# Two x tiles of a fused attention and gated-MLP kernel: by one DMA transpose in place of a load and eight TensorE transposes

## The chip, the cores and the metric

One core of one Trainium2 chip. The metric is the time of one execution on the device, in microseconds (us). Each kernel is run several times; all runs that are compared here were in the fast, undisturbed state, except that the state of e8_before_again, a single run, is unknown. The runs e0 to e3, e4 to e7 and e8 to e11 were made on three different chips, each group beside runs of the kernel before on the same chip; a ratio is always to these. A profile is one execution with its trace; the span in it is about 1.7 us shorter than the time on the device.

Names used below: TensorE (PE, with its weight loads as PEld), VectorE (DVE), ScalarE (ACT), GpSimd (POOL), SyncE (SP). A "q" after an engine's name is its sequencer: SPq is SyncE issuing DMAs.

## The reference, cut to what matters

```python
# x: [1, 2048, 512] bf16.  g * A(x) + (1 - g) * B(x), g = sigmoid(x @ gate_w)
def _B_ref(x, w_in, w_sp, b_sp, w_out):          # the gated MLP
    z = gelu(x @ w_in)                           # w_in: [512, 1376]; two halves of 688
    z1 = z[..., :688]
    z2 = layernorm(z[..., 688:])
    g = einsum('ts,bsf->btf', w_sp, z2) + b_sp[None, :, None]
    return (z1 * g) @ w_out
def _A_ref(x, wqkv, w_phi, wo): ...              # linear attention, 32 heads of 16; w_phi folded into q and k
```

Every product with x needs x transposed (features on the partitions) as the stationary operand. x has 16 tiles of 128 rows.

## The kernel before

The head loads x tiles 0 to 3 plainly into `xs`, transposes them on TensorE through PSUM, and takes tiles 4 to 15 by DMA transposes into `xT`. The z2 half of `w_in` comes in five pieces; the order in which TensorE needs them in the head is slab 0 (first part), slab 1, slab 2, slab 3, slab 0 (second part).

```python
    nc.sync.dma_start(out=xs[:, 0, :], in_=x2[0:P, :])
    nc.scalar.dma_start(out=w_z2[:, 0, 0:HF], in_=w_in_v[:, 0, FH:FH + HF])     # slab 0, first part
    nc.sync.dma_start(out=xs[:, 1, :], in_=x2[P:2 * P, :])
    load_z2w(nc.scalar, 1)                                                      # slab 1
    nc.sync.dma_start(
        out=xs[:, 2:4, :], in_=x2[2 * P:4 * P, :].rearrange("(i p) d -> p i d", p=P))
    load_z2w(nc.scalar, 2)                                                      # slab 2
    nc.sync.dma_start(out=w_z2[:, 0, HF:FH], in_=w_in_v[:, 0, FH + HF:F])       # slab 0, second part
    load_z2w(nc.scalar, 3)                                                      # slab 3
    x_dma_T(4)                      # DMA transpose of 128 rows
    for h in range(2):
        nc.sync.dma_start(out=w_z1[:, 2 * h:2 * h + 2, :], ...)
    for i in range(5, 8):
        x_dma_T(i)
    for q in range(2, NCH):
        nc.sync.dma_start_transpose(out=xT[:, :, q * CH:(q + 1) * CH], ...)     # 512 rows each
    # ... all on SyncE, in this order: brow, wqkT (2 transposes), wphi (8), wv_sb (2), wspT (4 transposes)
```

```python
    def z2_first_two():             # z2 of tiles 0 and 1; TensorE's program order
        # ... warm-up matmuls, transposes of tiles 0 and 1, products with slabs 0 and 1
        gate_T()                    # a matmul that turns gate_w into column 688 of w_z2
        one(0, 2, 0)                # first product with slab 2
        one(1, 2, 0)
        for dt in range(1, 3):
            one(0, dt, 1)
            one(1, dt, 1)
        x_T(2, 0, NDT, pq_tile([P, NDT, P], BF16)[:, :, :])      # four transposes, one copy
        for tt in range(2):
            one(tt, 3, 0)           # slab 3
            one(tt, 0, 1)           # slab 0, second part
            one(tt, 3, 1)
            z2_out(tt, zps[tt])     # ScalarE: gelu out of PSUM; VectorE: statistics
        x_T(3, 0, NDT, pq_tile([P, NDT, P], BF16)[:, :, :])
    # then z2_tile(2), z2_tile(3), z1 of tiles 0 to 3, z2 and z1 of tiles 4 to 15;
    # among tiles 8 to 11 the first "fold": 64 small matmuls on wqkT and wphi
```

The softmax here doesn't subtract the row's maximum and nothing guards it: scores larger than these inputs give would overflow.

## Time and profile before

| | |
|---|---|
| time before, first three runs | 208.83 us median (208.50 to 208.91) |
| TensorE busy | 201.7 of 206.8 us |
| first z2 matmul of tile 2 | 8.72 us |
| first matmul of the attention stage | 45.48 us |

From the page of the kernel before, its busy line and its chain of work that ended last:

```profile
PE 201.7 (98%) x1526; PEld 120.9 (58%) x1544; DVE 129.5 (63%) x278; ACT 76.5 (37%) x123; POOL 45.4 (22%) x73
...
PE 94%; DMA 2%; ACT 1%; issue 1%; ACTq 0%; DVE 0%
```

The view of waits, for TensorE alone (who waited for whom: us in total, times, longest):

```profile
PE zp L221 <- PEq L585: 0.8, 1, 0.8
PE zp L190 <- DMA w_z<-in_B_w_in_dram: 0.3, 1, 0.3
```

So TensorE runs nearly without a break, and what is cut from it, or from its waits, at the head should come off the total, as long as nothing later absorbs it. The timeline of the head (start, length, engine, line, operation; L190 are z matmuls, L276 transposes of x, L205 the gelu out of PSUM):

```profile
6.00 0.20 PE L286 MATMUL pq<-ident,gaterow 128*128 128x4 bf16 x1
...
6.52 1.04 PE L190 MATMUL zp<-w_z,xT 128*128 128x344 bf16 x6 [0.32 <-DMA w_z<-in_B_w_in_dram]
...
7.40 0.39 PE L276 MATMUL pq<-ident,xs 128*128 128x128 bf16 x4
...
7.62 1.04 PE L190 MATMUL zp<-w_z,xT 128*128 128x344 bf16 x6
...
8.50 0.39 PE L276 MATMUL pq<-ident,xs 128*128 128x128 bf16 x4
...
8.72 3.38 PE L190 MATMUL zp<-w_z,xT 128*128 128x344 bf16 x22
10.09 0.74 ACT L205 ACTIVATE z2all<-zp 128x688 bf16<-128x688 f32 x1 [0.46 <-PE zp L190]
```

Read starts, not lengths: a group of four transposes is 0.39 us long, but the next z matmul starts 0.22 us after the group does. The 10.09 is the gelu of tile 2.

SyncE's issues in the same timeline, and the landing of two loads from the list of DMA issues in the window from 1.7 to 3.3 us (KB each, median us from issue to landing):

```profile
1.74 0.43 SPq L123 DMA_DIRECT2D xs<-in_A_x_dram  x1
...
2.21 0.47 SPq L126 DMA_DIRECT2D w_z<-in_B_w_in_dram  x1
...
3.47 1.29 SPq L130 DMA_TRANSPOSE xT<-in_A_x_dram  x1
...
5.93 3.81 SPq L130 DMA_TRANSPOSE xT<-in_A_x_dram  x3
```

```profile
w_z<-in_B_w_in_dram ACTq DMA_DIRECT2D x3, 172.0 KB, 4.7
xs<-in_A_x_dram SPq DMA_DIRECT2D x1, 256.0 KB, 5.2
```

### The profile page before, as it was taken

The page shows a single profiled execution, that of the slowest core. Times are in us where ns is not written, and L with a number is a line of the kernel's source. Part 1 is how long each engine was busy: PE and PEld are TensorE (multiplying, and loading weights), DVE is VectorE, ACT ScalarE, POOL GpSimd, SP SyncE. Part 2 cuts the span into 40 slices and gives each one's busy share as a digit, 9 for nine tenths or more (in the row PEclk, how much of TensorE's full clock was granted, in tenths as well). Part 3 has the DMA queues.
Part 4 walks back from the last instruction along what each step waited for, and adds up shares of the span by engine and source line. Part 5 has one row for each costly group of instructions (what it writes and reads, how often), then busy time and mean ns, then how long its engine had stood idle before and what let it go on. Part 6 is the DMA issues. An engine that isn't in the chain of part 4 may idle for free.

```text
span 206.8 us, 3948 instructions
## 1 busy us (share of the span) xinstructions
PE 201.7 (98%) x1526; PEld 120.9 (58%) x1544; DVE 129.5 (63%) x278; ACT 76.5 (37%) x123; POOL 45.4 (22%) x73
## 2 busy tenths in 40 slices
PE   8999999999999999999999999999999999999994
PEld 4666666655566555556565666555455555655642
DVE  3377656656977778879797788555466553633330
ACT  2665678786322232333323032222251126001322
POOL 5020202020532327243342422222204220200000
PEclk9999999999999999999999999999999999999999
DMA  5999499999996025991413229763564767453642
GB/s 181 278 224 177 102 242 203 250 174 279 165 290 138 3 38 123 290 118 27 89 26 66 51 38 104 142 123 72 107 158 89 79 104 190 55 104 73 128 90 78
DMA packets 89315, 27.22 MB, mean 132 GB/s; under 512 B 83184, under 2 KB 89296, under 8 KB 89296
## 3 DMA queue, kind: packets, MB, share of 16 engines
q1 hardware_dynamic: 86384, 24.28, 62.8%
q10 hardware_dynamic: 2880, 2.68, 4.0%
q8 instruction: 12, 0.20, 0.4%
q14 instruction: 7, 0.06, 0.1%
q0 software_dynamic: 32, 0.00, 0.0%
HBM read 4.41 MB, written 2.10 MB: 31 GB/s over the span
## 4 chain that ended last, share of the span: by engine, by line
PE 94%; DMA 2%; ACT 1%; issue 1%; ACTq 0%; DVE 0%
PE mm L445 36%; PE zp L190 17%; PE mm L350 13%; PE mm L484 8%; PE mm L390 7%; PE mm L482 7%; DMA w_z<-in_B_w_in_dram 2%; PE at L458 2%; PE kvacc L406 2%; PE mm L487 1%; PE zp L303 0%; ACT z1all L256 0%; ACT wq_p L310 0%; ACTq L117 0%; PE pq L276 0%
## 5 line engine op out<-in xcount | busy, mean ns | idle before, releaser
L445 PE MATMUL mm<-z2all,wspT 128*128 128x344 bf16 x512 | 79.9, 309 | 0.0
L445 PEld LDWEIGHTS <-wspT 128*128 128x128 bf16 x512 | 49.0, 98 | 25.7 <-issue 0.4
L190 PE MATMUL zp<-w_z,xT 128*128 128x344 bf16 (+1 forms) x256 | 39.3, 312 | 0.3 <-DMA w_z<-in_B_w_in_dram 0.3
L354 ACT ACTIVATE eq<-mm 128x512 bf16<-128x512 f32 x32 | 17.4, 594 | 51.3 <-PE mm L350 21.3
L358 DVE TENSOR_REDUCE zs<-eq 128x64 f32<-128x1024 bf16 x16 | 19.5, 1220 | 20.4 <-ACT eq L354 20.4
L190 PEld LDWEIGHTS <-xT 128*128 128x128 bf16 x256 | 24.8, 99 | 12.4 <-issue 0.4
L450 DVE SCALAR_TENSOR_TENSOR ucat<-mm,bT,z1all 128x344 bf16<-128x344 f32 x32 | 17.4, 543 | 21.9 <-PE mm L445 21.9
L367 POOL TENSOR_TENSOR eq<-eq,ratio 128x512 bf16<-128x512 bf16 x16 | 16.9, 1059 | 49.9 <-DVE ratio L366 41.7
L354 ACT ACTIVATE ek<-mm 128x512 bf16<-128x512 f32 x32 | 17.3, 600 | 27.4 <-PE mm L350 27.4
L498 ACT ACTIVATE ob<-mm,g_inv 128x512 bf16<-128x512 f32 (+1 forms) x16 | 10.9, 681 | 32.8 <-PE mm L487 28.0
L358 DVE TENSOR_REDUCE zs<-ek 128x64 f32<-128x1024 bf16 x16 | 19.3, 1209 | 2.8 <-ACT ek L354 2.8
L484 PE MATMUL mm<-wspT,uT 128*128 128x512 bf16 (+2 forms) x85 | 20.1, 366 | 0.0
L350 PEld LDWEIGHTS <-xT 128*128 128x128 bf16 x128 | 12.2, 98 | 13.2 <-PE mm L487 0.8
L367 POOL TENSOR_TENSOR ek<-ek,ratio 128x512 bf16<-128x512 bf16 x16 | 16.9, 1059 | 2.3 <-DVE ratio L366 1.8
L350 PE MATMUL mm<-wq_p,xT 128*128 128x512 bf16 x55 | 16.0, 379 | 0.5
L390 PE MATMUL mm<-wv_sb,xT 128*128 128x512 bf16 x64 | 16.4, 379 | 0.0
L350 PE MATMUL mm<-wk_p,xT 128*128 128x512 bf16 x61 | 16.1, 379 | 0.3
L482 PE MATMUL mm<-wspT,oT 128*128 128x512 bf16 (+2 forms) x62 | 15.6, 365 | 0.3
L208 DVE BATCH_NORM_STATS2 bn<-z2all 128x6 f32<-128x344 bf16 x32 | 14.9, 501 | 0.0
L205 ACT ACTIVATE z2all<-zp 128x688 bf16<-128x688 f32 x16 | 11.8, 744 | 6.9 <-PE zp L190 6.9
L256 ACT ACTIVATE z1all<-zp 128x688 bf16<-128x688 f32 x16 | 11.9, 744 | 5.1 <-PE zp L190 4.6
L484 PEld LDWEIGHTS <-uT 128*128 128x128 bf16 x85 | 8.1, 98 | 9.2
(72 smaller groups left out, 145.2 us busy)
## 6 DMA issues: line engine op xcount, KB each, us to landing
out_dram<-ob ACTq DMA_DIRECT2D x15, 128.0 KB, 1.7
wspT<-in_B_w_out_dram SPq DMA_DIRECT2D x2, 640.0 KB, 4.8
w_z<-in_B_w_in_dram SPq DMA_DIRECT2D x2, 344.0 KB, 4.3
w_z<-in_B_w_in_dram ACTq DMA_DIRECT2D x3, 172.0 KB, 4.7
wv_sb<-in_A_wqkv_dram SPq DMA_DIRECT2D x2, 256.0 KB, 3.5
wspT<-in_A_wo_dram SPq DMA_DIRECT2D x2, 256.0 KB, 3.8
xs<-in_A_x_dram SPq DMA_DIRECT2D x2, 128.0 KB, 2.6
xs<-in_A_x_dram SPq DMA_DIRECT2D x1, 256.0 KB, 5.2
```

The costliest lines, as they stand in the source:

```text
L190: nc.tensor.matmul(zp[:, j, 0:n], lhsT=xT[:, dt, tt * P:(tt + 1) * P], rhs=wt[:, dt, j * HF:j * HF + n], start=(dt == first), stop=(dt == ...
L208: nc.vector.bn_stats(out=bn6[:, tt, j, :], in_=z2v[:, j, :])
L256: nc.scalar.activation(out=z1all[:, tt, :].rearrange("p (j n) -> p j n", j=2), in_=zp[:, :, 0:HF], func=AF.Gelu_apprx_tanh,)
L350: nc.tensor.matmul(ps[:, :], lhsT=xT[:, dt, tt * P:(tt + 1) * P], rhs=w[:, dt, :], start=(dt == 0), stop=(dt == NDT - 1))
L354: nc.scalar.activation(out=e[:, :, a, :], in_=ps[:, :].rearrange("p (h f) -> p h f", f=DH), func=AF.Exp, scale=1.0 - 2.0 * a)
L358: nc.vector.tensor_reduce(out=z[:].rearrange("p h a -> p (h a)"), in_=e[:].rearrange("p h a f -> p (h a) f"), axis=AX.X, op=ALU.add,)
L367: nc.gpsimd.tensor_tensor(out=e[:, :, 1, :], in0=e[:, :, 1, :], in1=ratio[:, :, None].to_broadcast([P, H, DH]), op=ALU.mult)
L390: nc.tensor.matmul(v_ps[:, :], lhsT=xT[:, dt, tt * P:(tt + 1) * P], rhs=wv_sb[:, dt, :], start=(dt == 0), stop=(dt == NDT - 1))
L445: nc.tensor.matmul(gp[:, 0:HF], lhsT=wspT[:, st, tt * P:(tt + 1) * P], rhs=z2all[:, st, j * HF:(j + 1) * HF], start=(st == 0), stop=(st == ...
L450: nc.vector.scalar_tensor_tensor(out=ucat[tt % NU][:, c0 + j * HF:c0 + (j + 1) * HF], in0=gp[:, 0:HF], scalar=bT[:, tt:tt + 1], in1=z1all[ ...
L482: nc.tensor.matmul(acc, lhsT=oT[:, g, :], rhs=wo_t[:, g, c0:c1], start=(g == 0), stop=False)
L484: nc.tensor.matmul(acc, lhsT=uT[:, i + ft, :], rhs=w_main[i][:, ft, c0:c1], start=False, stop=False)
```

## The change

The intent: take 0.45 us of transposes off TensorE at the head, where it is the bound, and let the DMA queues do them beside it.

```diff
-    xs = early.tile([P, 4, D], BF16, name="xs")
+    xs = early.tile([P, 2, D], BF16, name="xs")
@@
-    nc.sync.dma_start(
-        out=xs[:, 2:4, :], in_=x2[2 * P:4 * P, :].rearrange("(i p) d -> p i d", p=P))
     load_z2w(nc.scalar, 2)
     nc.sync.dma_start(out=w_z2[:, 0, HF:FH], in_=w_in_v[:, 0, FH + HF:F])
     load_z2w(nc.scalar, 3)
-    def x_dma_T(i):
-        nc.sync.dma_start_transpose(out=xT[:, :, i * P:(i + 1) * P], in_=x2[i * P:(i + 1) * P, :])
-    x_dma_T(4)
+    def x_dma_T(i, n=1):
+        nc.sync.dma_start_transpose(out=xT[:, :, i * P:(i + n) * P], in_=x2[i * P:(i + n) * P, :])
+    x_dma_T(2, 2)
     # (the two w_z1 loads)
-    for i in range(5, 8):
+    for i in range(4, 8):
         x_dma_T(i)
@@ z2_first_two
-        x_T(2, 0, NDT, pq_tile([P, NDT, P], BF16)[:, :, :])
         for tt in range(2): ...
-        x_T(3, 0, NDT, pq_tile([P, NDT, P], BF16)[:, :, :])
```

## The prediction

> **What bounds the kernel now.** TensorE. The page's busy table has PE at 201.7 us of a 206.8 us span, and its chain that ended last is 94% PE. The list of waits for PE has two entries: 0.8 us at the start and 0.3 us (once) for a load of w_z at 6.52 us. So only PE time at the head, or a wait there, can change the total.
>
> **What the change removes.**
> - Eight TensorE transposes (x tiles 2 and 3) and their two PSUM copies. The groups show a transpose at 219 ns, but these overlap. The timeline gives the real cost: the first group starts at 7.40 us and the next z matmul at 7.62; the second at 8.50, the next z matmul at 8.72. That is 0.22 us each, 0.45 us together, all on the chain. It agrees with about 56 ns from start to start of warm 128-column matmuls (the Trainium skill, "TensorE: Matmul & The Clock Gate", section "Wait — 56ns, not 53.3ns?"): 4 x 56 = 0.22 us. The VectorE copies (0.42 and 0.41 us) are off the chain.
> - The 256 KB load of xs tiles 2 and 3, issued at 1.74 us, 5.2 us to landing, ahead of the last part of w_z on SyncE.
>
> **What it adds and moves.** One 256-row DMA transpose, SyncE's fourth DMA, at about 2.2 us. The first transpose DMA of before waited on SyncE for a w_z landing (0.8 us in SyncE's list of waits, start 3.47): it is the ninth DMA and reuses a semaphore. The new one is the eighth and should not wait. Issue took 1.27 us for 128 rows and 1.88 us for 512; I estimate 1.45 us, so issue ends near 3.7. The single transposes of tiles 4 to 7 end issue near 9.7 us, as before; the w_z1 loads go out about 1 us earlier.
>
> **When does it land?** Ahead of it are 944 KB of loads instead of 1200 KB. Transpose packets in the trace are 256 bytes and take about 18 ns; 1024 of them over 16 DMA engines are about 1.15 us (estimate). The loads of before moved their first 944 KB by about 5.3 us; adding 1.15 us and some 0.5 us from last packet to landing gives about 7.0 us. Plausible: 6.6 to 8.0. PE needs tile 2 at about 8.0 to 8.3 us, so I expect no wait, with a margin near 1 us.
>
> **A second gain.** DMA queues are served in turn, packet by packet (the Trainium skill, "DMA: Bandwidth & Descriptors", section "Queues, rings and completion order"). With small 256-byte packets later in place of xs 2 and 3, the w_z slab that PE waited for (landed 6.48) should land near 6.1, so the 0.3 us wait should mostly vanish: the gate matmul before it runs at 6.00. I count 0.15 us.
>
> **Later.** Downstream DMAs have slack: the last w_phi load lands at 24.5 us, its matmuls start at 27.5; the first w_sp quarter lands at 36.7, used at 48.1. Nothing should take the gain back.
>
> **Sum.** 208.83 - 0.45 - 0.15 = 208.2 us. Range 207.7 to 208.8. Faster over 2%: 0.01. Same: 0.98. Slower over 2%: 0.01.
>
> **What would show it.** The timeline: first z2 matmul of tile 2 at about 8.1 us instead of 8.72; the fourth SyncE issue at about 2.2 us, landing near 7.0; no PE wait for xT; the w_z wait at most 0.1 us; everything after earlier by a constant 0.6 us.
>
> **What would make it wrong.** The transpose landing after 8.2 us (PE waits, gain halved or lost); its packets delaying the third or fourth w_z slab (needed near 6.2 and 7.2 us; landed 6.48 and 7.44 before); a longer issue; or a later wait that absorbs the gain.

## The result, and the profile after

Ratios here are the mean time of one kernel's runs over the mean of the other's in the same rounds, so not quite the ratio of the medians quoted beside them.

| | before | after | ratio (95% interval) |
|---|---|---|---|
| first comparison, 4 and 4 runs | 208.67 | 207.80 | 0.9960 (0.9942 to 0.9979) |
| e0_after_again, 11 and 6 runs | 208.64 | 208.01 | 0.9968 (0.9948 to 0.9987) |
| e11_after_third, 11 and 6 runs | 208.34 | 207.76 | 0.9967 (0.9940 to 0.9994) |

The three ratios are worth 0.8, 0.7 and 0.7 us of 208.6 us. By the rule of 2% that is "same"; the gain is small, but it is there in all three. Single runs scatter: those of before from 207.90 to 209.39 us, those of the changed kernel from 207.03 to 208.70.

From the page after:

```profile
PE 202.2 (98%) x1536; PEld 120.3 (58%) x1536; DVE 128.8 (62%) x276; ACT 76.5 (37%) x123; POOL 45.4 (22%) x73
...
PE 95%; DMA 2%; ACT 1%; ACTq 0%; DVE 0%; issue 0%
```

PE's busy sum has not fallen although eight instructions are gone: the trace of before lacks some matmul records (1526 listed, 1536 after; the weight loads, 1544 and 1536, do show the eight), which is why starts are compared here and not sums.

TensorE's waits after:

```profile
PE zp L219 <- PEq L581: 0.8, 1, 0.8
PE zp L188 <- DMA w_z<-in_B_w_in_dram: 0.2, 1, 0.2
```

The timeline after (L188 are the z matmuls, L203 the gelu), then SyncE's issues and the landing of the new transpose:

```profile
6.00 0.18 PE L282 MATMUL pq<-ident,gaterow 128*128 128x4 bf16 x1
...
6.41 5.57 PE L188 MATMUL zp<-w_z,xT 128*128 128x344 bf16 x37 [0.23 <-DMA w_z<-in_B_w_in_dram]
...
9.53 0.74 ACT L203 ACTIVATE z2all<-zp 128x688 bf16<-128x688 f32 x1 [0.23 <-PE zp L188]
```

```profile
1.74 0.42 SPq L124 DMA_DIRECT2D w_z<-in_B_w_in_dram  x1
...
2.21 1.57 SPq L128 DMA_TRANSPOSE xT<-in_A_x_dram  x1
...
3.83 1.08 SPq L132 DMA_DIRECT2D w_z<-in_B_w_in_dram  x2
...
4.96 5.27 SPq L128 DMA_TRANSPOSE xT<-in_A_x_dram  x4
```

```profile
xT<-in_A_x_dram SPq DMA_TRANSPOSE x1, 5.7
```

From 6.41 us on, the z matmuls run without a break: no transposes, no wait for `xT`. Tile 2's gelu starts at 9.53 instead of 10.09 us, 0.56 us earlier: 0.11 because slab 2 released TensorE at 6.41 instead of 6.52, 0.45 because of the transposes. The attention stage's first matmul is at 44.93 instead of 45.48 us (TensorE's timelines of before and after, in this order), and the span is 0.5 us shorter.

```profile
45.48 0.81 PE L350 MATMUL mm<-wk_p,xT 128*128 128x512 bf16 x2
```

```profile
44.93 1.24 PE L346 MATMUL mm<-wk_p,xT 128*128 128x512 bf16 x5
```

In these two traces the whole difference arises before 8.2 us and is carried to the end unchanged.

But SyncE's transposes of tiles 4 to 7 end their issue at 10.23 us (4.96 + 5.27) instead of 9.75. That will matter below.

### The profile page after: what moved, and what is told of

The parts are those of the page before. It is cut to its first block, busy times and chain, and to the rows that moved or that the text cites. A ratio compares the mean times of both kernels' runs of the same rounds, so it can differ in the third digit from the quotient of the medians.

```text
span 206.3 us, 3946 instructions
## 1 busy us (share of the span) xinstructions
PE 202.2 (98%) x1536; PEld 120.3 (58%) x1536; DVE 128.8 (62%) x276; ACT 76.5 (37%) x123; POOL 45.4 (22%) x73
## 4 chain that ended last, share of the span: by engine, by line
PE 95%; DMA 2%; ACT 1%; ACTq 0%; DVE 0%; issue 0%
PE mm L441 36%; PE zp L188 17%; PE mm L346 14%; PE mm L480 8%; PE mm L478 7%; PE mm L386 7%; DMA w_z<-in_B_w_in_dram 2%; PE at L454 2%; PE kvacc L402 2%; PE mm L483 1%; PE zp L299 0%; ACT z1all L252 0%; ACT wq_p L306 0%; ACTq L117 0%; ACTq L120 0%; PE pq L299 0%
## 5 line engine op out<-in xcount | busy, mean ns | idle before, releaser
L188 PE MATMUL zp<-w_z,xT 128*128 128x344 bf16 (+1 forms) x256 | 38.9, 312 | 0.2 <-DMA w_z<-in_B_w_in_dram 0.2
L188 PEld LDWEIGHTS <-xT 128*128 128x128 bf16 x256 | 24.9, 98 | 12.4 <-issue 0.3
L478 PE MATMUL mm<-wspT,oT 128*128 128x512 bf16 (+2 forms) x68 | 16.6, 366 | 0.0
L203 ACT ACTIVATE z2all<-zp 128x688 bf16<-128x688 f32 x16 | 11.8, 744 | 6.3 <-PE zp L188 6.3
```

The costliest lines, as they stand in the source:

```text
L188: nc.tensor.matmul(zp[:, j, 0:n], lhsT=xT[:, dt, tt * P:(tt + 1) * P], rhs=wt[:, dt, j * HF:j * HF + n], start=(dt == first), stop=(dt == ...
L478: nc.tensor.matmul(acc, lhsT=oT[:, g, :], rhs=wo_t[:, g, c0:c1], start=(g == 0), stop=False)
```

## The experiments

The theories. **A**, that of the prediction: two parts, 0.45 us of TensorE time in the head and some tenths because slab 2 lands earlier, and nothing later takes them back. Rivals: **R1**, the gain is the lighter DMA head and the transposes hide behind it; **R2**, the gain is the two VectorE copies that vanish; **R3**, the new transpose has slack; **B**, there is a third source of gain, since the first medians differ by more than the traces. Theories **C** and **D** came up on the way.

This table has, for each trace, the times that the argument uses, read from starts and landings in the traces: when slab 2 landed, when TensorE began on it, when tile 2's first z2 matmul started, how long it was from there to the end of the last matmul, and the time of that run.

| trace | slab 2 landed | TensorE goes on | tile 2 starts | difference | tile 2 to last matmul | that run |
|---|---|---|---|---|---|---|
| before | 6.48 | 6.52 | 8.72 | 2.20 | 195.27 | 208.54 |
| e8_before_again | 5.64 | 5.78 | 8.29 | 2.52 | 195.26 | 208.09 |
| after | 6.37 | 6.41 | 8.16 | 1.75 | 195.26 | 208.00 |
| e0_after_again | 5.67 | 5.71 | 7.46 | 1.75 | 195.27 | 207.28 |
| e11_after_third | 6.01 | 6.05 | 7.80 | 1.75 | 195.51 | 207.89 |
| e1_idle_T | 6.08 | 6.12 | 8.32 | 2.20 | 195.26 | 208.12 |
| e2_idle_T_copies | 6.26 | 6.30 | 8.74 | 2.44 | 195.25 | 208.53 |
| e3_before_swap | 6.57 | 6.61 | 9.21 | 2.59 | 195.24 | 208.99 |
| e4_drop_T_only | 7.01 | 7.05 | 8.84 | 1.78 | 195.25 | 208.64 |
| e5_late | 7.46 | 7.51 | 10.91 | 3.40 | 195.29 | 210.73 |
| e6_split | 5.93 | 5.97 | 7.73 | 1.75 | 195.93 | 208.34 |
| e7_reorder_split | 5.74 | 5.78 | 7.53 | 1.75 | 196.26 | 208.48 |
| e9_split_chunk_late | 5.96 | 6.07 | 8.06 | 2.00 | 195.36 | 208.10 |
| e10_reorder_chunk_late | 5.25 | 5.66 | 7.56 | 1.90 | 195.24 | 207.50 |

From tile 2 to the end the kernel takes 195.24 to 195.29 us in ten of the fourteen traces, whatever the head did. So the head decides, except in e11, e6, e7 and e9.

The two traces of before and the three of the changed kernel, set against each other by their means: tile 2 starts 0.70 us earlier (8.50 and 7.81), as much as the measured gain. Of this, 0.09 us is an earlier start on slab 2 and 0.61 us a shorter stretch from there to tile 2: 0.45 of transposes, and 0.16 that is the mean of what e8 alone lost in it (see e8). With so few traces this is an account, not a measurement.

### The changed kernel again, twice: e0_after_again, e11_after_third

No edit.

> The changed kernel unaltered, for a tighter difference and a second trace. Theory A (eight transposes leave TensorE, 0.45 us, and the w_z wait shrinks by 0.1 us, everything else carried along): 0.55 us below before. Theory B (there is a further gain of 0.3 us somewhere, as the first medians, 0.87 us apart, suggest): 0.8 to 0.9 us below before. Tile 2's first z matmul again near 8.16 us and the 256-row transpose landing near 7.9 us.

> The changed kernel once more, in the same rounds as the two versions above, to compare with them. 0.6 to 0.9 us below before; w_phi lands at 24.7 to 25.4 us, 1.6 us ahead of the fold; tile 2's transpose lands 0.1 to 0.6 us ahead of need.

Measured: ratios 0.9968 and 0.9967, as in the table above. Tile 2 starts at 7.46 and 7.80 us, not again at 8.16: the landing of slab 2 differs by 0.7 us between executions of one kernel. The transpose landed at 7.18 and 7.71 us, 0.28 and 0.10 us before tile 2's first matmul. In e11 nothing was left: tile 2's weight load, which in after and e0 starts 0.145 us ahead of its matmul (8.02 and 7.32 us), started only at 7.75, 0.055 us ahead, just in time for the matmul. The gain of 0.7 us lies between theories A (0.55) and B (0.8 to 0.9), and the intervals hold both, so the times do not decide. The traces need no third source: the first profiled run of the changed kernel was its slowest of four, with a late head. In e11 w_phi landed at 26.66 us, where 24.7 to 25.4 was expected, 0.04 us after the fold had begun; that trace lost time there (see theory D).

### Transposes put back on TensorE: e1_idle_T, e2_idle_T_copies

```diff
+    def idle_T(i):
+        tp = pq_tile([P, NDT, P], BF16)
+        for dt in range(NDT):
+            nc.tensor.transpose(tp[:, dt, :], xs[:, i, dt * P:(dt + 1) * P], ident[:, :])
+        # e2 only:
+        with tc.high_priority():
+            nc.vector.tensor_copy(out=spare[:, :, i * P:(i + 1) * P], in_=tp[:, :, :])
@@ z2_first_two, where x_T(2, ...) and x_T(3, ...) stood before
+        idle_T(0)
+        idle_T(1)
```

> The changed kernel with eight TensorE transposes put back where they were, into PSUM that nobody reads; TensorE's program is then that of before. Theory A: 0.45 us slower than the changed kernel, so 0.1 us below before. Rival R1 (the gain is the lighter DMA head, transposes on TensorE hide): as fast as the changed kernel. Rival R2 (the gain is the VectorE copies that vanish): as fast as the changed kernel too, and the next run then slower.

> As e1_idle_T, and the two 128x512 VectorE copies put back as well, into a spare tile; the programs of TensorE and VectorE are those of before and only the DMAs differ. Theory A: equal to e1_idle_T within 0.1 us, 0.1 us below before. Rival R2 (copies on VectorE cost): 0.3 us or more slower than e1_idle_T.

Measured: e1 208.17 us (ratio to before 0.9981, 0.9962 to 1.0000), e2 208.37 us (0.9988, 0.9969 to 1.0008); the changed kernel in the same rounds 208.01 us. By means, e1 and e2 are 0.26 and 0.43 us above the changed kernel and 0.42 and 0.26 us below before. Taken together, their twelve runs are 0.35 us above the changed kernel's six and 0.34 us below before's eleven, each good to about 0.3 us by the scatter of the runs (95%). The timeline of e1:

```profile
6.12 1.04 PE L188 MATMUL zp<-w_z,xT 128*128 128x344 bf16 x6 [0.48 <-DMA w_z<-in_B_w_in_dram]
...
6.99 0.39 PE L285 MATMUL pq<-ident,xs 128*128 128x128 bf16 x4
...
8.32 3.67 PE L188 MATMUL zp<-w_z,xT 128*128 128x344 bf16 x24
```

From 6.12 to 8.32 us is 2.20 us again, as before; without the transposes it is 1.75. R1 falls: the transposes do not hide, they cost 0.45 us of TensorE in the trace, and the times agree, within their scatter. R2 is not supported: e2 with the copies is 0.16 us above e1, which the scatter covers, and e2's trace has 2.44 us because the first two matmuls of that stretch took 445 and 447 ns instead of 307: TensorE's clock was released only at 6.81 us in that execution.

What e1 and e2 keep of the change is its DMAs alone. That is worth 0.3 us on average, though each run's own interval just reaches or includes no gain at all. So the lighter DMA head is likely a part of the gain; what the runs refuse is that it is the whole.

### Only the order of two loads: e3_before_swap

```diff
-    nc.sync.dma_start(out=xs[:, 2:4, :], ...)
     load_z2w(nc.scalar, 2)
     nc.sync.dma_start(out=w_z2[:, 0, HF:FH], ...)
+    nc.sync.dma_start(out=xs[:, 2:4, :], ...)
```

> The kernel before with only the order of two loads on SyncE exchanged: the last part of w_z's first slab third, the 256 KB load of xs tiles 2 and 3 fourth. Theory A: the slab of w_z that TensorE waits for lands no later than 6.4 us, the 0.3 us wait becomes 0.1 to 0.2 us, the total 0.1 us below before. Rival R1 (load order is the gain): 0.5 us or more below before. The xs load must land by 7.3 us or TensorE waits for it.

Measured: 208.83 us, ratio 1.0013 (0.9990 to 1.0036). No gain. In its trace slab 2 landed at 6.57, slab 3 at 7.87 and the xs load at 7.83 us, 0.4 us after TensorE wanted it: TensorE waited for it before its transposes (2.59 us in the table instead of 2.20). The exchange alone does not bring the gain; it moves the wait to the xs load.

### Transposes taken out, DMAs of before: e4_drop_T_only

```diff
-        x_T(2, 0, NDT, pq_tile([P, NDT, P], BF16)[:, :, :])
-        x_T(3, 0, NDT, pq_tile([P, NDT, P], BF16)[:, :, :])
+        next_turn("pq", 2)              # in place of each: keeps the turn of the PSUM buffers
+    def xw(dt, tt):                     # tiles 2 and 3 read as 0 and 1: wrong on purpose
+        t = tt - 2 if tt in (2, 3) else tt
+        return xT[:, dt, t * P:(t + 1) * P]
-            lhsT=xT[:, dt, tt * P:(tt + 1) * P]
+            lhsT=xw(dt, tt)             # in all matmuls
```

> The kernel before with the eight transposes and their two copies taken out and no DMA changed; x tiles 2 and 3 are read as tiles 0 and 1, so the result is wrong on purpose. The compute engines run exactly the programs of the changed kernel, SyncE and its DMAs exactly those of before. Theory A (two additive parts, 0.45 us of transposes and 0.2 to 0.4 us of earlier w_z): 0.45 us below before, and from TensorE's release by w_z to the first matmul of tile 2 takes 1.75 us instead of 2.20. Rival R1 (the gain is the lighter DMA head): as slow as before.

Measured: the result was wrong, as meant; 208.59 us, ratio 1.0003 (0.9972 to 1.0034), so inconclusive: the interval holds both the expected 0.9978 and no gain. One run of the six, 210.43 us, had a mean TensorE clock of 0.992; without it the mean is 208.43 us, 0.2 us below before. Its trace:

```profile
7.05 5.02 PE L194 MATMUL zp<-w_z,xT 128*128 128x344 bf16 x33 [0.50 <-DMA w_z<-in_B_w_in_dram]
```

The stretch has shrunk from 2.20 to 1.78 us, as expected, but it starts at 7.05, since slab 2 landed at 7.01; and slab 3 and the second part of slab 0 landed at 7.92 and 7.91 us, so late that TensorE, now faster, waited 0.03 us for them. So in this trace taking the transposes out gave 0.42 of their 0.45 us, and what kept its total up is the late slab 2. But with the DMAs of before, the later pieces of w_z stand right behind the transposes as the next bound, and in e8 they would have cost more: there the second part of slab 0 landed at 7.30 us with five matmuls of 0.146 us to follow before tile 2, so without transposes tile 2 could not have started before 8.03 us (an estimate from these two numbers), 0.26 us earlier than it did. So the two parts of the change need not simply add up: by the estimate from e8, the lighter DMAs make room for a part of the 0.45 us. The landings fit: slab 3 landed at 6.88 to 7.92 us in the four traces with the xs load (before, e8, e3, e4) and at 6.33 to 7.01 us in five with the transpose (after, e0, e11, e1, e2); the second part of slab 0 at 7.30 to 7.91 and 5.50 to 6.57 us (6.36 in e3, where it is issued ahead of the xs load).

### The new transpose later: e5_late

```diff
-    x_dma_T(2, 2)
     for h in range(2):
         nc.sync.dma_start(out=w_z1[:, 2 * h:2 * h + 2, :], ...)
+    x_dma_T(2, 2)
```

> The changed kernel with the 256-row transpose issued sixth on SyncE, behind the two 344 KB w_z1 loads. Theory A (its landing is only just ahead of need: 7.88 against 8.02 us): it lands near 9.5 us, TensorE waits 1.2 to 1.8 us for it, and the total is 1.2 to 1.8 us above the changed kernel. Rival R3 (the landing has slack, the 1 us margin of the prediction, and later stages absorb the rest): no more than 0.5 us above.

Measured: 209.78 us, ratio 1.0056 (1.0029 to 1.0084); 1.2 us above before, so, with the changed kernel 0.7 us below before in other rounds, about 1.9 us above it. The size is just above what theory A expected, 1.2 to 1.8 us, and the way is another. The profiled run (the slowest, 210.73 us):

```profile
6.48 0.18 PE L282 MATMUL pq<-ident,gaterow 128*128 128x4 bf16 x1 [0.97 <-DMA gaterow<-in_gate_w_dram]
...
7.51 4.47 PE L188 MATMUL zp<-w_z,xT 128*128 128x344 bf16 x18 [0.85 <-DMA w_z<-in_B_w_in_dram]
```

TensorE waited 0.97 us for the gate row and 0.85 us for slab 2, and its clock records show half speed from 7.55 to 10.96 us: a z matmul took 495 ns instead of 310. The transpose landed at 10.38, ahead of tile 2 at 10.91, so in this trace it was not what TensorE waited for. The edit also put the two 344 KB w_z1 loads ahead of it, next to the z2 weights in the queues, and the likely reading is that they delayed what the head needs at once. The stretch of 3.40 us in the table is 1.65 us longer than in the changed kernel, all by the half clock; the other three runs, not traced, had a mean clock of 0.998 or more and averaged 209.59 us, 0.9 us above before. So the edit changes two things, and its time says nothing on R3, whether the transpose's landing has slack: that is read from the traces of the changed kernel (0.10 to 0.28 us, and a weight load that waited in e11), not from here.

### Two transposes in place of one, and another order of slabs: e6_split, e7_reorder_split

```diff
-    x_dma_T(2, 2)
+    x_dma_T(2)
+    x_dma_T(3)
# e7 only:
-    load_z2w(nc.scalar, 2)
-    nc.sync.dma_start(out=w_z2[:, 0, HF:FH], in_=w_in_v[:, 0, FH + HF:F])
+    load_z2w(nc.sync, 2)
     load_z2w(nc.scalar, 3)
+    nc.scalar.dma_start(out=w_z2[:, 0, HF:FH], in_=w_in_v[:, 0, FH + HF:F])
```

> The changed kernel with two 128-row transposes, fourth and fifth on SyncE, in place of one of 256 rows. Theory A: TensorE's critical path is the same, so within 0.15 us of the changed kernel; tile 2 lands about 0.5 us before its need instead of 0.14 us, tile 3 later but before its own need 1.2 us after; the w_z1 loads go out 1 us later and still land in time.

> As e6_split, and the third slab of w_z (the one TensorE waits for) goes third on SyncE, the last part of the first slab last on ScalarE's queue. Theory A: that slab lands near 5.5 us instead of about 6.1, TensorE is released by the gate row or the earlier matmuls instead, and the total is 0.1 to 0.4 us below the changed kernel. Rival R4 (the head is bound by the sum of its bytes): another slab or tile 2 becomes the wait, and the total stays within 0.1 us.

Measured: 208.80 us (ratio 1.0004, 0.9984 to 1.0025) and 208.86 us (1.0022, 0.9999 to 1.0045). Both lose the whole gain, and both expectations missed. The head did as theory A said: tile 2 landed at 6.97 and 6.80 us and started at 7.73 and 7.53. But from tile 2 to the end took 195.93 and 196.26 us instead of 195.26. TensorE's waits of e6, and SyncE's issue of w_phi in its timeline:

```profile
PE pq L300 <- DMA wphi<-in_A_w_phi_dram: 0.5, 1, 0.5
```

```profile
22.10 3.81 SPq L148 DMA_DIRECT2D wphi<-in_A_w_phi_dram  x8
```

The same issue in before and in after:

```profile
19.20 4.01 SPq L149 DMA_DIRECT2D wphi<-in_A_w_phi_dram  x8
```

```profile
20.20 3.98 SPq L147 DMA_DIRECT2D wphi<-in_A_w_phi_dram  x8
```

SyncE issues everything in one row, and each 128-row transpose keeps it about 1.25 us. The second one pushes all that follows back: w_phi, issued from 20.20 us on in after, is issued from 22.10 us on here and lands at 27.11 us, while the fold began at 26.54. TensorE stood in the fold. Not all of the 1.90 us is the second transpose itself: the single transposes end 0.88 us later than in after (11.11 and 10.23 us), and the rest comes from the longer issue of the transposes behind them (5.26 us for the two of 512 rows, 4.49 in after). Why these took longer is not shown. e7 is the same, w_phi at 27.23 and the fold from 26.35. The waits view names another engine for TensorE's 0.8 us there, but for the weight loads it names w_phi:

```profile
PEld L300 <- DMA wphi<-in_A_w_phi_dram: 0.9, 1, 0.9
```

R4 is neither shown nor refused by e7, since its loss lies at the fold.

This gave **theory D**: the change draws on a slack that I had not counted, the time by which w_phi lands before the fold. By the traces it was 3.03 us (27.54 - 24.51) and 2.10 us in the two traces of before, 1.62, 1.60 and -0.04 us in the three of the changed kernel, and -0.57 and -0.88 in e6 and e7. It shrinks from both sides: the faster head brings the fold forward, and w_phi is issued later. In e0 it is nearly all the first: w_phi lands at 24.68 us, even before that of e8 (25.01), but the fold begins 0.83 us sooner.

### The last x transpose behind w_phi: e9_split_chunk_late, e10_reorder_chunk_late

```diff
-    for q in range(2, NCH):
-        nc.sync.dma_start_transpose(out=xT[:, :, q * CH:(q + 1) * CH], ...)
+    x_chunk(2)
     # (brow, wqkT, wphi)
+    x_chunk(3)
     # (wv_sb, wspT)
```

> e6_split with the last 512-row x transpose moved on SyncE from before the w_phi loads to behind them. Theory D (e6_split lost 0.5 to 0.9 us at the fold at 26.5 us, because its SyncE queue brings w_phi at 27.1 us): w_phi lands near 24.5 us, no wait at the fold, 0.5 to 0.8 us faster than e6_split, at or up to 0.2 us below the changed kernel. Rival (the split costs something at the head): no faster than e6_split.

> e7_reorder_split with the same move. Theory D: no wait at the fold, 0.7 to 1.0 us faster than e7_reorder_split; 0 to 0.3 us below the changed kernel if the earlier third slab of w_z is worth anything.

Measured: 207.92 us (ratio 0.9969, 0.9949 to 0.9990) and 208.11 us (0.9976, 0.9954 to 0.9999), beside 207.76 us (0.9967) for the changed kernel in the same rounds. SyncE in e9:

```profile
18.96 4.05 SPq L150 DMA_DIRECT2D wphi<-in_A_w_phi_dram  x8
```

w_phi lands at 24.18 us, 2.7 us before the fold at 26.88, and TensorE's waits no longer list it. From ratio 1.0004 to 0.9969 and from 1.0022 to 0.9976 are 0.7 and 1.0 us: theory D holds, with w_phi's landing and the time both as it said. Neither version beats the changed kernel, though; its slab order and its 256-row transpose are as good, and earlier slab 2 (5.25 us in e10) buys little, since TensorE is then held by the gate matmul at 5.64 us, and 0.15 us more two matmuls later, where the copy of the gate's result is needed. The 0.1 us that e9 takes more between tile 2 and the end arises at the end of the second fold, at 37.5 us by its trace; what held TensorE there is not shown.

In e11, the changed kernel itself, the same thing begins. The fold's 64 weight loads in the timelines of after and of e11, in this order:

```profile
26.97 0.56 PEld L299 LDWEIGHTS <-wqkT 32*128 32x128 bf16 x64 [0.28 <-issue]
```

```profile
26.62 0.71 PEld L299 LDWEIGHTS <-wqkT 32*128 32x128 bf16 x64 [0.28 <-issue]
```

0.56 us in one, 0.71 in the other, where w_phi landed at 26.66 us, 0.04 us after the fold's first weight load; that trace takes 0.25 us more from tile 2 to the end than the others, 0.14 of it here and 0.11 at the end of the second fold, at 37.4 us, as in e9.

### The kernel before again: e8_before_again

> The kernel before, unaltered, for a second trace of it. Theory C (the third w_z slab lands later, 6.48 to 7.01 us, where 1024-byte packets of the xs load stand on SyncE's queue beside it, and earlier, 5.67 to 6.37 us, where 256-byte transpose packets do): it lands at 6.4 us or later. If it lands before 6.2 us, the second part of the gain is not shown.

Measured: one run, 208.09 us, among the faster of before. Slab 2 landed at 5.64 us, so **theory C falls**: the range of landings with the plain xs load (5.64 to 7.01 us) covers that with the transpose (5.67 to 6.37 us in five traces, without the late and reordered versions). And the wait shows up elsewhere:

```profile
5.78 1.15 PE L190 MATMUL zp<-w_z,xT 128*128 128x344 bf16 x6
...
6.94 0.23 PEld L276 LDWEIGHTS <-xs 128*128 128x128 bf16 x4 [0.37 <-DMA xs<-in_A_x_dram]
6.94 0.40 PE L276 MATMUL pq<-ident,xs 128*128 128x128 bf16 x4
...
8.29 3.67 PE L190 MATMUL zp<-w_z,xT 128*128 128x344 bf16 x24
```

Although TensorE went on at 5.78 us, it then waited for the xs load (landed 6.90 us) before transposing tile 2. The 0.37 us are idle time of the weight loads; the matmuls lost 0.18 us by it, since the transposes, due 0.146 us after the matmul at 6.62, started at 6.94 instead of 6.76. Another 0.11 us went earlier in the same stretch, where the third matmul waited for the copy of the gate's result (6.18 instead of 6.07); together they are most of the 0.32 us by which its stretch exceeds 2.20. Before has two gates in its head, slab 2 and the load of tiles 2 and 3, and in each of its two traces one of them was late; the first profile showed only slab 2, because TensorE was released so late there that the xs load, landed at 6.94 us, was in time.

## Why the prediction was right or wrong

- **Level and direction: right, the level in part by luck.** 208.2 us was predicted with 207.7 to 208.8, and 207.8 measured (207.76 to 208.01 in three comparisons). The predicted gain was 0.6 us, the measured one 0.7 to 0.8. But the range was wider than the gain: the later medians of before itself, 208.67, 208.64 and 208.34 us, lie in it too, so that the level fell into it proves little. What speaks for the prediction is the difference and the 0.45 us in the traces; that the 0.15 us added for slab 2 brought the sum close to the measured gain is in part luck, as the third point shows.
- **"0.22 us each, 0.45 us together, all on the chain": right.** 2.20 us against 1.75 us in every trace without another wait, and back to 2.20 in e1. It was read from starts of matmuls; the lengths, 219 ns each, would have given 1.8 us for eight.
- **"The w_z slab that PE waited for should land near 6.1, so the 0.3 us wait should mostly vanish": the step that is not shown.** In the traces of the changed kernel it landed at 6.37, 5.67 and 6.01 us, in those of before at 6.48 and 5.64, so one execution differs from the next by more than the effect. What the DMAs alone bring, by e1 and e2 against before, is 0.26 to 0.42 us with intervals that touch zero (0.34 us, give or take 0.3, together), and at least one way it comes is another than predicted: the wait for the load of xs tiles 2 and 3, which cost TensorE's matmuls 0.18 us in e8, is gone. How much is which stays open.
- **"About 7.0 us ... a margin near 1 us": mis-sized.** The 256-row transpose landed at 7.88, 7.18 and 7.71 us, 0.28, 0.28 and 0.10 us before tile 2's first matmul. My sum added its packets to the end of the loads before it; in the trace of the changed kernel its packets are spread from 4.4 to 7.4 us between those of the w_z slabs on the other queue (which agrees with queues served in turn), and the two DMA queues together moved 32 to 68 KB per quarter of a microsecond from 4.25 to 6.75 us, against 88 to 94 KB from 7.75 to 9.25 us, when only w_z1 was left (counted from the trace's packet records, each packet spread over the time that it took). The stated range, 6.6 to 8.0, held.
- **"The single transposes of tiles 4 to 7 end issue near 9.7 us, as before" and "nothing should take the gain back": wrong, though it cost little.** Issue of the 256 rows took 1.57, 1.32 and 1.80 us (1.45 estimated), the singles ended at 10.23, 9.92 and 10.48 us, and in e11 w_phi, behind them on SyncE, landed 1.7 to 2.2 us later than in the traces of before (the singles account for 0.7 to 0.9 us of this, longer issues of the transposes behind them for most of the rest). The slack of 3 us that the prediction named shrank to 1.6 us and once to nothing, and in e6 and e7, where w_phi landed 0.6 to 0.9 us after the fold had begun, the whole gain was gone.

## What to carry to other kernels

Where TensorE is the bound, moving work off it pays at its start-to-start time, and only where the loads that stand behind it come early enough to be used: look at every landing within the next microsecond, not only at the wait that the profile lists. A DMA transpose is paid for in the issuing queue too; before adding one, follow that queue to the end of the stage and list by how much each later transfer lands ahead of its use. One trace is one draw: with 0.7 us between executions at the head, take two or three traces of each kernel before a tenth is explained.

## What the Trainium skill lacked or had wrong

- "TensorE: Matmul & The Clock Gate", section "What's actually happening", says that the moment of the clock's release varies by about 500 ns either way. Here the same warm-up, from 0.85 us on, was released between 3.97 and 6.81 us in thirteen traces. That is a spread of 2.84 us, within the page's free-running window of 3.4 us, and the window itself agrees: the half-speed stretch in e5 lasted 3.41 us.
- The same page, section "Why this matters for your kernels", warns of idle gaps above about 3 us. In e5 two gaps of 0.97 and 0.85 us, 0.2 us apart, were followed by half the clock from 7.55 us on. One gap of 0.83 us at e7's fold was not, so a single gap of this length did not do it there; no run here shows the limit.
- The same page, "Part 4: PE-mode transpose", gives 275 to 390 ns for one transpose and says that the full clock does not engage for its transpose mode. Here a transpose is 219 ns long, but four in a row start 56 ns apart at the full clock and cost 0.22 us (the trace lists them as matmuls, the x tile as weights and the identity as the other operand, and does not tell whether that mode was on), in agreement with the section "Wait — 56ns, not 53.3ns?" of the page.
- "DMA: Bandwidth & Descriptors" has sequencer times for a DMA transpose of small tiles and for one within SBUF, but does not say how long the issuing engine is held by a load from HBM as its rows grow: on SyncE 1.2 to 1.4 us for 128 rows of 512 elements (2.0 once, in e5), 1.3 to 1.9 us for 256, 1.7 to 3.0 us for 512. This had its part in e6 and e7.
